# K read like V: 32 heads by four rows in 4 MB transfers, and a TensorE loop that branches to its slot

## Chip, cores and metric

One core of a Trainium2 chip runs the whole program. The metric is the device time of one execution in microseconds; the kernel before takes 214.04 us, the median of three runs.

## What is computed

A decode step with one query per sequence (batch 4): attention over a window of a K and V cache, plus a small MLP block on the same normalised input. Cut to what matters:

```python
B, D = 4, 576
Hq, Hkv, Sk, Dh, W = 32, 16, 8192, 128, 2048      # bf16
xn = layernorm(x)
q  = (xn @ wq).reshape(B, 32, 128)
k, v = k_cache[:, :, Sk-W:, :], v_cache[:, :, Sk-W:, :]   # 16 heads, each used by two query heads
p  = softmax(q . k / sqrt(128))                    # per query head, over 2048 rows
A  = (p @ v).reshape(B, 4096) @ wo
h  = gelu(layernorm(xn) @ w1)                      # sequence length 1: the shifts of h leave zeros
x1 = xn + shifted(h) @ w2
out = x + A + x1 + gelu(layernorm(x1) @ w3) @ w4
```

The K window is 4 x 16 x 2048 x 128 bf16, 33.55 million bytes, and V the same. With wq, wo, w1 to w4 the core reads 88.49 MB.

## The kernel before

**Engines and order.** Each engine runs a list written out ahead: `add(engine, emit, waits, sig, key)` puts an operation down, the lists are sorted by `key`, and an operation waits for named signals of others. TensorE has three such lists and two hardware loops between them: list `pe` (projections and MLP up to the hidden layer), the K loop (L653), list `pe2` (softmax's transposes), the V loop (L674), list `pe3` (output).

**DMA.** SP issues all large transfers from one list (L199, `add_dma`) in the order w1, w2, wq, w3, K, V, w4, wo. A transfer waits on SP for its slot to come free, and what stands behind it on SP waits too. Two buffers, `kring` (four slots of 2 MB and a rest) and `vring` (five slots of 2 MB), are shared by weights, K, V and the output weights in turn: wq lies in kring's second half until `q`, w3 in vring until `h2_1`.

**K.** `kv_src` reads K in 16 chunks of 2 MB, one sequence and four heads each: a partition row is 64 successive cache rows of one head, 16 KB. Four slots in kring; chunk c waits until the transposes of chunk c-4 are done. One turn of the K loop takes four chunks, one slot each, so that every instruction has its slot's address fixed; four turns.

For every chunk TensorE transposes 64 blocks of 128 x 128 (L485, eight to a PSUM bank, with `perm_bf` as the moving operand), VectorE (L469) and ScalarE (L468) copy the banks to `ktb` in the ratio 5 to 3, and TensorE multiplies (L492): four quarters by four heads, each 32 weight columns by 512 moving columns, written to one of four column groups of the array. The product of chunk c stands after the third block of chunk c+1. The weights are `Qs`, 128 columns that VectorE copies from `Qpad` for each chunk (L474). `Qpad` holds every head's two queries in its own columns with zeros beside them, so that the products of all chunks add up in four PSUM banks (`Sps`), which a zeroing of four products (L347) has prepared. All scores of the kernel stand there at the end, one partition for each query head of each sequence.

**Softmax.** VectorE takes the maximum over 2048 columns of PSUM (L498), ScalarE makes four exponentials of 512 columns (L502), VectorE transposes each in 32 x 32 blocks (L520), TensorE sorts them with 0/1 weights `pick_bf` in 64 products (L514), and two copies each on VectorE and ScalarE (L526, L529) put the result into `PT_t`.

**V.** Eight transfers of 4 MB, each with two sequences of 16 heads by four partitions: a partition row is 128 successive cache rows, 32 KB. Four slots: both halves of `vring`'s first 8 MB, then of kring's. VectorE spreads the probabilities (L545), TensorE multiplies (L553). The fifth transfer waits for the first's products, and so on; w4 waits for the sixth's products, wo for the fifth's and sixth's.

**End.** The products with w4 and wo (L392) are added up as the weights land, and two copies and one small DMA give the output.

Of the kernel before, what the change touches and what calls it, by code (L numbers as in the profile page):

```python
# [5 lines left out]
FP32 = mybir.dt.float32  # L6
# [8 lines left out]
N_LOOP = 4  # L15
N_CB = 4
# [21 lines left out]
def bass_parallel_sum__sliding_block_cached__mixer_s_mlp__decode_kernel(  # L38
# [16 lines left out]
    assert N_LOOP * N_CB == NC and LB % 4 == 0 and LB % NKT == 0  # L55
# [5 lines left out]
    CH = [(b, gq) for gq in range(4) for b in range(B)]  # L61
# [8 lines left out]
    with ExitStack() as ctx:  # L70
# [11 lines left out]
        kslot_t = lambda s: kslot(s).rearrange("p (t d) -> p t d", t=NT)  # L82
        vslot = lambda k: (vring, vring, kring, kring)[k][:, k % 2 * 2 * UE:(k % 2 + 1) * 2 * UE]
        ktbuf = ktb[:].rearrange("p (s t d) -> p s t d", s=NKT, t=8)
        ktgrp = ktb[:].rearrange("p (s t u i) -> p s t u i", s=NKT // 2, t=16, u=NU)
# [20 lines left out]
        PTx = vring[:, 4 * UE:4 * UE + 4 * 512].rearrange("p (q x) -> p q x", q=4)  # L106
# [22 lines left out]
        Qs = sb("Qs", [128, N_CB, 128], BF16)  # L129
        ident_bf = sb("ident_bf", [128, 128], BF16)  # L130
        perm_bf = sb("perm_bf", [128, 128], BF16)
        permT_bf = sb("permT_bf", [128, 128], BF16)
        pick_bf = sb("pick_bf", [128, 2 * NVS, 2, 32], BF16)
# [9 lines left out]
        negb = sb("negb", [128, 1], FP32)  # L143
        rs4 = sb("rs4", [128, 4], FP32)
# [11 lines left out]
        Sps = ps[:, 0:4, :]  # L156
# [21 lines left out]
        S["PV"] = sem("pv")  # L178
        S["FO"] = sem("fold")
# [57 lines left out]
        pool_ident(perm_bf, "perm_bf", [[-1, NU], [-NU, NI]], perm_bf[:].rearrange("p (u i) -> p u i", u=NU), -94)  # L237
        pool_ident(permT_bf, "permT_bf", [[-1, NI], [-NI, NU]], permT_bf[:].rearrange("p (i u) -> p i u", u=NU), -93)
        P(lambda e: e.memset(ktb[:, NKT // 2 * 1024:NKT * 1024], 0.0), key=-92, inc=(("E", LB - 2), 1))  # L239
        P(lambda e: e.memset(Qs[:, N_CB - 1, :], 0.0), key=-91, inc=(("E", LB - 1), 1))  # L240
        for j in (LB - 4, LB - 3):
            P(lambda e, j=j: e.sem_inc(S["E", j], 1), key=-90)
# [3 lines left out]
        P(lambda e: e.memset(pick_bf[:], 0.0), sig="pick0", key=-86)  # L246
        for gl in range(2):
            pick_v = pick_bf[:, :, gl, 16 * gl:16 * gl + 16]
            P(lambda e, v=pick_v: e.memset(v, 1.0), waits=["pick0"], sig=f"pick1{gl}", key=-85 + 0.1 * gl)
        for gl in range(2):  # L250
            for x in range(2 * NVS):
                v = pick_bf[:, x, gl, 16 * gl:16 * gl + 16].rearrange("p (u r) -> p u r", u=NU)
                P(lambda e, v=v, x=x: e.affine_select(out=v, in_=v, compare_op=ALU.is_equal, fill=0.0, base=-(8 * (x // 2) + x % 2),
                                                      pattern=[[-NI, NU], [-2, 4]], channel_multiplier=1),
                  waits=["pick11"], sig=f"pick2{gl}{x}", key=-84 + 0.1 * (8 * gl + x))
# [23 lines left out]
        def v_src(c, t0, t1):  # L279
# [5 lines left out]
        t_done = lambda c: f"T{NBLK * c + NBLK - 1}"  # L285
# [367 lines left out]
        with nc.Fori(0, N_LOOP, engines=[PE]) as it:  # L653
# [64 lines left out]
```

## Time and profile before

| | |
|---|---|
| median of three runs | 214.04 us (213.75 to 214.1) |
| the profiled execution | 213.93 us, of which the span from first to last instruction is 212.6 us |
| busy: TensorE, VectorE, ScalarE, GpSimd | 172.5, 111.9, 58.6, 15.6 us |
| bytes read | 88.49 MB, 416 GB/s over the span |
| K, V transfers | 16 of 2 MB; 7 of 4 MB and 2 of 2 MB |
| mean granted TensorE clock | 0.928 |

Lines below are those of the profile's page or of its views. A group's row has the kernel's line, engine, operation, what it writes and reads, shapes and count, then busy microseconds and mean nanoseconds of one, then idle time before it and what ended that. A row of the chain in order of time has start and duration in microseconds and what. A row of the view by windows has the stretch and its length, the busy time of TensorE, its weight loads, VectorE, ScalarE and GpSimd, the granted clock, the DMA engines' busy share and the GB/s. Matmuls overlap, so a mean of one is longer than the distance from one to the next.

### The profile page before, as it was taken

What the parts mean: (1) busy time and instruction counts of PE and PEld (TensorE: products, weight loads), DVE (VectorE), ACT (ScalarE), POOL (GpSimd) and SP (SyncE); (2) the same over time, 40 slices, a digit from 0 to 9 for tenths busy, and PEclk for the clock granted to TensorE, in tenths of its full rate; (3) what the DMA queues carried; (4) which work ended last, traced back from release to release, by engine and by line L of the source; (5) the groups of instructions that cost most, each with busy time, mean ns of one, the idle gap of its engine ahead of it and who ended that gap; (6) DMA issues with size and microseconds to landing.
All of it is one profiled execution on the core that took longest, in us unless ns stands there. A gap on an engine that the chain in (4) does not pass through costs nothing.

```text
span 212.6 us, 4856 instructions
## 1 busy us (share of the span) xinstructions
PE 172.5 (81%) x2212; PEld 133.7 (63%) x2216; DVE 111.9 (53%) x168; ACT 58.6 (28%) x69; POOL 15.6 (7%) x38
## 2 busy tenths in 40 slices
PE   1456147999999999999996089999989598997495
PEld 0222014888878888887774048988868487883262
DVE  5433200477776777777764869995575444003000
ACT  2004001366665566666656520000000000000000
POOL 8991000000000000000000000000000000000000
PEclk9997855899999999999999589999999889999799
DMA  6999999999999999999999999999999999999993
GB/s 242 453 444 445 429 396 416 432 425 427 429 416 438 432 422 429 435 422 424 432 444 438 444 407 459 413 425 453 407 444 438 419 425 410 451 476 393 407 408 131
DMA packets 5066, 88.65 MB, mean 417 GB/s; under 512 B 568, under 2 KB 704, under 8 KB 1216
## 3 DMA queue, kind: packets, MB, share of 16 engines
q1 hardware_dynamic: 5040, 88.49, 97.7%
q8 instruction: 8, 0.13, 0.3%
q14 instruction: 2, 0.02, 0.0%
q10 hardware_dynamic: 16, 0.01, 0.0%
HBM read 88.49 MB, written 0.00 MB: 416 GB/s over the span
## 4 chain that ended last, share of the span: by engine, by line
DMA 47%; PE 45%; DVE 4%; SPq 1%; ACT 1%; issue 1%
PE ps L485 23%; DMA vring<-in_A_wo_dram 15%; DMA vring<-in_B_w_dram 13%; DMA vring<-in_A_v_cache_dram 12%; PE ps L553 11%; DMA kring<-in_A_k_cache_dram 7%; PE ps L492 6%; PE ps L430 2%; SPq L199 1%; DVE vring L520 1%; DVE rmax L498 1%; DVE ktb L545 1%; PE ps L514 1%; PE ps L347 1%; ACT ktb L468 0%
## 5 line engine op out<-in xcount | busy, mean ns | idle before, releaser
L469 DVE COPY ktb<-ps 128x1024 bf16<-128x1024 bf16 x80 | 53.8, 689 | 23.5 <-PE ps L485 23.4
L485 PEld LDWEIGHTS ps<-perm_bf,kring 128*128 128x128 bf16 x1024 | 58.2, 98 | 8.3 <-issue 7.6
L485 PE MATMUL ps<-perm_bf,kring 128*128 128x128 bf16 x1024 | 61.7, 220 | 0.2
L468 ACT ACTIVATE ktb<-ps 128x1024 bf16<-128x1024 bf16 x48 | 48.0, 1023 | 32.5 <-PE ps L485 32.1
L545 DVE TENSOR_TENSOR ktb<-kring,mH_bf 128x4096 bf16<-128x4096 bf16 x16 | 36.2, 2286 | 14.6 <-PE ps L553 14.6
L553 PE MATMUL ps<-vring,ktb 128*128 128x256 bf16 x256 | 30.3, 282 | 4.3 <-DMA vring<-in_A_v_cache_dram 3.5
L553 PEld LDWEIGHTS ps<-vring,ktb 128*128 128x128 bf16 x256 | 25.7, 101 | 8.5 <-issue 3.6
L553 PE MATMUL ps<-kring,ktb 128*128 128x256 bf16 x256 | 28.6, 273 | 0.9 <-DMA kring<-in_A_v_cache_dram 0.9
L553 PEld LDWEIGHTS ps<-kring,ktb 128*128 128x128 bf16 x256 | 25.0, 98 | 4.5 <-issue 1.1
L608 ACT ACTIVATE out_sb<-ps 4x288 bf16<-4x288 f32 x1 | 0.4, 399 | 84.6 <-PE ps L392 84.6
L492 PE MATMUL ps<-ktb,Qs 128*32 128x512 bf16 x272 | 17.8, 382 | 1.2 <-ACT ktb L468 1.2
L430 PE MATMUL ps<-vring,xs 128*8 128x320 bf16 (+1 forms) x72 | 4.5, 429 | 7.6 <-DMA vring<-in_B_w_dram 7.6
L492 PEld LDWEIGHTS ps<-ktb,Qs 128*32 128x32 bf16 x272 | 5.7, 96 | 6.7 <-DVE ktb L469 1.4
L514 PE MATMUL ps<-vring,pick_bf 128*32 128x256 bf16 x64 | 3.9, 411 | 6.4 <-DVE rinv L532 6.4
L609 DVE CAST out_sb<-ps 4x288 bf16<-4x288 f32 x1 | 0.4, 449 | 15.7 <-PE ps L392 15.7
L392 PE MATMUL ps<-vring,h2T_sb 128*4 128x288 bf16 x72 | 6.2, 347 | 3.1 <-DMA vring<-in_B_w_dram 3.1
L571 DVE TENSOR_SCALAR tmp<-ps,maskd 128x128 f32<-128x128 f32 x2 | 0.7, 350 | 14.8 <-PE ps L553 14.8
L430 PEld LDWEIGHTS ps<-vring,xs 128*8 128x8 bf16 x72 | 2.1, 110 | 9.8 <-DMA vring<-in_B_w_dram 8.0
L330 PE MATMUL ps<-ident_bf,xp_bf 4*128 4x4 bf16 x15 | 0.8, 163 | 8.1 <-DVE xp_bf L314 5.0
L392 PEld LDWEIGHTS ps<-vring,h2T_sb 128*4 128x4 bf16 x72 | 3.7, 101 | 5.8 <-DMA vring<-in_B_w_dram 3.6
L514 PEld LDWEIGHTS ps<-vring,pick_bf 128*32 128x32 bf16 x64 | 2.0, 118 | 8.2 <-DVE rinv L532 6.9
L239 POOL MEMSET ktb<- 128x8192 bf16 x1 | 6.9, 6924 | 0.0
(93 smaller groups left out, 78.6 us busy)
## 6 DMA issues: line engine op xcount, KB each, us to landing
kring<-in_A_k_cache_dram SPq DMA_DIRECT2D x16, 2048.0 KB, 13.8
vring<-in_A_v_cache_dram SPq DMA_DIRECT2D x4, 4096.0 KB, 24.6
kring<-in_A_v_cache_dram SPq DMA_DIRECT2D x3, 4096.0 KB, 34.0
vring<-in_B_w_dram SPq DMA_DIRECT2D x2, 5184.0 KB, 25.1
kring<-in_A_wq_dram SPq DMA_DIRECT2D x1, 4608.0 KB, 15.7
kring<-in_A_v_cache_dram SPq DMA_DIRECT2D x2, 2048.0 KB, 27.4
vring<-in_A_wo_dram SPq DMA_DIRECT2D x1, 1872.0 KB, 26.9
vring<-in_A_wo_dram SPq DMA_DIRECT2D x1, 1440.0 KB, 29.8
```

The lines of the kernel that those rows point to most:

```text
L199: e.dma_start(o_, i_).then_inc(S[skey], 16)
L239: P(lambda e: e.memset(ktb[:, NKT // 2 * 1024:NKT * 1024], 0.0), key=-92, inc=(("E", LB - 2), 1))
L347: ins = e.matmul(ps[:, w, :], lhsT=zeros_bf[:, 0:128], rhs=zeros_bf[:, :], start=True, stop=True)
L392: return e.matmul(ACC[h], lhsT=lhsT, rhs=rhs, start=start, stop=stop, tile_position=(0, 32 * h), skip_group_check=True)
L430: ins = e.matmul(H2ps[k][32 * j:32 * j + 2 * B].rearrange("b (p t) -> b p t", t=n), lhsT=x_at(2, s_), rhs=w[:, :, 9 * j + t0:9 * j + t0 + ...
L468: return "act", lambda e: e.activation(out=ktbuf[:, n % NKT], in_=tb[n % 4], func=ACTF.Copy)
L469: return "dve", lambda e: e.tensor_copy(out=ktbuf[:, n % NKT], in_=tb[n % 4])
L485: ins = e.transpose(tb[j % 4][:, t, :], kslot_t(k)[:, 8 * kb + t, :], perm_bf[:])
L492: ins = e.matmul(Sps[32 * u:32 * u + 32, q, :].rearrange("p (t i) -> p t i", t=16), lhsT=Qs[:, k, 32 * u:32 * u + 32], rhs=ktgrp[:, (4 * k ...
L514: ins = e.matmul(ps[32 * j:32 * j + 32, 4 + qt, 256 * ih:256 * (ih + 1)].rearrange("p (t a e) -> p t a e", a=NPAIR, e=2), lhsT=pick_bf[:, ...
L545: return lambda e: e.tensor_tensor(out=PTpad[:, n % 4], in0=PTv[:, qt, NH * h:NH * (h + 1), bp, :].unsqueeze(2).to_broadcast([128, NH, NX, ...
L553: ins = e.matmul(ps[:, 0, 0:256], lhsT=PTpad[:, 2 * (k % 2) + h, 2 * g:2 * g + 2].rearrange("p t h e -> p (t h e)"), rhs=vslot(k)[:, Dh * ...
```

## The change

K is read in eight transfers of 4 MB in V's form: two sequences of 16 heads, four rows of partitions per head, 128 cache rows in each. The first comes in two halves. There are three slots instead of four: both halves of kring, and vring's second 4 MB, which w3 holds at first; so the third transfer waits for `h2_1`, later ones for the transposes of the third before. The second V transfer now waits for K's sixth to be transposed. A GpSimd operation for each landing counts up one semaphore, `KL`, for which the loop waits.

One turn of TensorE's loop is now one transfer, two halves of eight blocks; eight turns. Since three slots do not divide the turns evenly, the slot is a register (`k_at`), and each half of the body stands three times, once for each slot, chosen by two nested conditions. The score products stand once for each half: 32 heads, 32 weight columns by 256 moving columns, the weights taken from a buffer with all heads of two sequences (copied twice in the run instead of 16 times). The moving operand has runs of four elements, 256 bytes apart; eight rounds of four column groups add up in one half bank. VectorE takes each half's scores from PSUM to `S_sb`: a copy for the first two sequences, an addition for the others, and a maximum for each finished quarter. The zeroing before the loop goes.

In the softmax the exponentials read `S_sb`; VectorE's transposes and the 64 products go, and 40 products with full weights (`sel_bf`) of P itself put the probabilities in place: 32 of 128 columns, quarter by quarter, for two banks, and 8 of 512 columns for the other two banks, which only the second pair of sequences needs.

```diff
-N_LOOP = 4
-N_CB = 4
+N_LOOP = 8
+N_CB = 2
+NKS = 3
...
+        S_sb = vring[:, 4 * UE:4 * UE + 4096].bitcast(FP32).rearrange("p (q x) -> p q x", q=4)
-        kslot = lambda s: kring[:, s * UE:(s + 1) * UE]
+        kslot = lambda k: (kring[:, 0:2 * UE], kring[:, 2 * UE:4 * UE], vring[:, 2 * UE:4 * UE])[k]
-        ktgrp = ktb[:].rearrange("p (s t u i) -> p s t u i", s=NKT // 2, t=16, u=NU)
+        ktgrp = ktb[:].rearrange("p (s t h i) -> p s t h i", s=2, t=NT, h=NX)
...
-        def kv_src(cache, c):
-            b, gq = CH[c]
-            return cache[b, NU * gq:NU * gq + NU, Sk - W:Sk, :].rearrange("g (i t) d -> i g (t d)", t=NT)
...
+        def kv_src(cache, c, t0=0, t1=NTV):
             bp, qt = VCH[c]
             k0 = Sk - W + 4 * NTV * qt
-            return A_v_cache[2 * bp:2 * bp + 2, :, k0:k0 + 4 * NTV, :].rearrange(
+            return cache[2 * bp:2 * bp + 2, :, k0:k0 + 4 * NTV, :].rearrange(
                 "b h (i t) d -> (b h) i (t d)", t=NTV)[:, :, Dh * t0:Dh * t1]
...
-        for c in range(NC):
-            w = [t_done(c - N_CB)] if c >= N_CB else (["q"] if c >= 2 else [])
-            add_dma([(kslot(c % N_CB), kv_src(A_k_cache, c))], ("k", c % N_CB), w, c)
+        t_done = lambda c: f"T{2 * NBLK * (c + 1) - 1}"
+        for c in range(NCK):
+            w = [t_done(c - NKS)] if c >= NKS else ([], ["q"], ["h2_1"])[c]
+            for n, (u0, u1) in enumerate([(0, NH), (NH, NTV)] if c == 0 else [(0, NTV)]):
+                ev_k = add_dma([(kslot(c % NKS)[:, Dh * u0:Dh * u1], kv_src(A_k_cache, c, u0, u1))], ("k", c % NKS) if n == 0 else "k0b", w, c + 0.1 * n)
+                if n == 0:
+                    P(lambda e: e.sem_inc(S["KL"], 1), waits=[ev_k], key=c)
         for c in range(NCV):
-            w = [f"PV{2 * (c - NVS) + 1}"] if c >= NVS else [t_done(NC - N_CB + 2 * c - 3)] if c >= 2 else ["h2_1"]
+            w = [f"PV{2 * (c - NVS) + 1}"] if c >= NVS else [t_done(NCK - NVS + c)] if c else ["h2_1"]
...
-        add("pe", pe_zero, waits=["h2T"], sig="s_zero", key=-9.5)
+        add("dve", lambda e: e.tensor_copy(out=Qs, in_=Qpad_t[:, 0:1024]), waits=["qT3"], sig="Qs0", key=0)
+        add("dve", lambda e: e.tensor_copy(out=Qs, in_=Qpad_t[:, 1024:2048]), waits=[f"SC{NC // 2 - 1}"], key=NB // 2 + NBLK - 0.4)
...
-                ins = e.transpose(tb[j % 4][:, t, :], kslot_t(k)[:, 8 * kb + t, :], perm_bf[:])
+                ins = e.transpose(tb[j % 4][:, t, :], kslot(k)[:, Dh * (8 * j + t):Dh * (8 * j + t + 1)], ident_bf[:])
...
-            for q in range(4):
-                for u in range(NU):
-                    ins = e.matmul(Sps[32 * u:32 * u + 32, q, :].rearrange("p (t i) -> p t i", t=16),
-                                   lhsT=Qs[:, k, 32 * u:32 * u + 32], rhs=ktgrp[:, (4 * k + q) % (NKT // 2), :, u, :],
-                                   start=False, stop=False, tile_position=(0, 32 * u), skip_group_check=True)
+            for h in range(NX):
+                u = h % NU
+                ins = e.matmul(ps[32 * u:32 * u + 32, k, 0:256].rearrange("p (t i) -> p t i", t=NT),
+                               lhsT=Qs[:, 32 * h:32 * h + 32], rhs=ktgrp[:, k, :, h, :],
+                               start=(h < NU), stop=(h >= NX - NU), tile_position=(0, 32 * u), skip_group_check=True)
...
+        S_at = lambda c: S_sb[:, c % 8 // 2, 256 * (c % 2):256 * (c % 2 + 1)]
+        for c in range(NC):
+            last = c == NC - 1
+            w, key = (["SCend"], KS) if last else ([f"SC{c}"], NBLK * (c + 2) - 0.5)
+            if c < NC // 2:
+                add("dve", lambda e, c=c: e.tensor_copy(out=S_at(c), in_=ps[:, c % 2, 0:256]), waits=w, key=key)
+            else:
+                add("dve", lambda e, c=c: e.tensor_tensor(out=S_at(c), in0=S_at(c), in1=ps[:, c % 2, 0:256], op=ALU.add), waits=w,
+                    sig="S_last" if last else f"S{c}", key=key)
+                if c % 2:
+                    add("dve", lambda e, c=c: e.tensor_reduce(out=rm4[:, c % 8 // 2:c % 8 // 2 + 1], in_=S_sb[:, c % 8 // 2, :], axis=AX.X, op=ALU.max),
+                        waits=["S_last" if last else f"S{c}"], sig="rm4" if last else None, key=key + 0.01)
...
-        def pe_PT(qt):
+        def pe_PT(q0, q1, x):
             def f(e):
                 ins = None
+                for i in range(4):
+                    ins = e.matmul(ps[:, 4 + x, 128 * q0:128 * q1].rearrange("p (q t) -> p q t", t=128), lhsT=sel_bf[:, x, 3 - i:131 - i],
+                                   rhs=P_sb[:, q0:q1, 128 * i:128 * (i + 1)], start=(i == 0), stop=(i == 3), skip_group_check=True)
                 return ins
             return f
...
         with nc.Fori(0, N_LOOP, engines=[PE]) as it:
             turn = e.snap(it + 1)
-            landed = e.snap(16 * it + 16)
+            k_at = e.snap(it * 32 - ((it * 11) & 96) * NKS, min_val=0, max_val=64)
 
             def wait(j):
-                if j % NBLK == 0:
-                    e.wait_ge(S["k", j // NBLK], landed)
+                if j == 0:
+                    e.wait_ge(S["KL"], turn)
+                if j == NBLK:
+                    e.wait_ge(S["k0b"], 16)
                 e.wait_ge(S["E", (j - 4) % LB], turn)
-            for j in range(LB):
-                emit_T(e, j, wait)
-                if j % NBLK == 2:
-                    k = (j // NBLK - 1) % N_CB
-                    e.wait_ge(S["E", NBLK * k + 6], turn)
-                    e.wait_ge(S["E", NBLK * k + 7], turn)
-                    emit_SC(e, k).then_inc(S["SC"], 1)
+
+            def half(h, k):
+                for j in range(NBLK * h, NBLK * (h + 1)):
+                    emit_T(e, j, wait, k)
+            for h in range(2):
+                with e.If(k_at < 32):
+                    half(h, 0)
+                with e.Else():
+                    with e.If(k_at < 64):
+                        half(h, 1)
+                    with e.Else():
+                        half(h, 2)
+                k = 1 - h
+                for x in (6, 7):
+                    e.wait_ge(S["E", NBLK * k + x], turn)
+                emit_SC(e, k).then_inc(S["SC"], 1)
```

More of the change, by code (lines that the diff above doesn't have):

```diff
@@ L342, in x_at @@
             return xs_t[:, idx, 2 * B * (s_ + 1):2 * B * (s_ + 2)]
-        def pe_zero(e):
-            ins = None
-            for w in range(4):
-                ins = e.matmul(ps[:, w, :], lhsT=zeros_bf[:, 0:128], rhs=zeros_bf[:, :], start=True, stop=True)
-            return ins
         ln_ops(0, x_sb, xn_bf, [ev_x], "ln1", -40)
@@ L472, in bass_parallel_sum__sliding_block_cached__mixer_s_mlp__decode_kernel @@
             c, k = n // NBLK, n % NBLK
-            if k == 0:
-                add("dve", lambda e, c=c: e.tensor_copy(out=Qs[:, c % N_CB, :], in_=Qpad_t[:, 128 * (4 * CH[c][0] + CH[c][1]):][:, 0:128]),
-                    waits=[f"SC{c - 2}"] if c >= 1 else ["qT3"], key=n)
             eng, f = evac(n)
```

89 lines of the change are left out of this document (40 added, 49 removed).

## Prediction

> **What bounds the kernel now.** I read the page's top and its DMA part first, then the DMA view cut to two stretches, then the chain that ended last, in order of time.
>
> ```profile
> span 212.6 us, 4856 instructions
> DMA  6999999999999999999999999999999999999993
> q1 hardware_dynamic: 5040, 88.49, 97.7%
> q8 instruction: 8, 0.13, 0.3%
> ```
>
> The 16 DMA engines are over 90% busy in every slice but the first and the last; 97.7% of the span on the one data queue leaves about 5 us, which is the start and the end. Everything read is 88.49 MB, and the change reads the same bytes. So the span is: a start, 88.49 MB at the engines' pace, an end. A faster compute engine gains nothing. There are two ways to move the time: make the engines move the bytes faster, or let them run dry.
>
> The chain, in order of time (start, duration, what):
>
> ```profile
> 2.17 27.46 DMA vring<-in_B_w_dram
> ...
> 35.49 0.32 DVE h2T_sb L452
> 35.81 0.45 issue
> 36.26 1.49 PE ps L347 x3
> ...
> 44.38 0.98 PE ps L492 x16
> 45.36 3.71 PE ps L485 x64
> ...
> 94.51 14.58 DMA kring<-in_A_k_cache_dram
> ...
> 115.17 1.07 PE ps L492 x16
> 116.27 2.30 DVE rmax L498
> ...
> 118.78 0.79 ACT Qpad L502 x2
> 119.59 2.72 DVE vring L520 x4
> ...
> 122.62 2.05 PE ps L514 x32
> 124.70 0.69 DVE kring L526
> 125.39 2.21 DVE ktb L545
> ...
> 127.73 7.16 PE ps L553 x64
> ...
> 142.08 25.49 DMA vring<-in_A_v_cache_dram
> ...
> 178.35 31.68 DMA vring<-in_A_wo_dram
> ```
>
> The chain is named 45% TensorE, but look at the three DMA pieces: 14.58, 25.49 and 31.68 us from issue to landing. 4 MB (4.194 million bytes) at about 0.43 MB/us take 9.75 us, so these transfers stood in a queue. The chain passes through their issue, yet an issue some microseconds later would have been absorbed by that queue. These waits are the slack that the change may spend.
>
> **The transfers.** K goes from 16 pieces of 2 MB, 16 KB in each partition row, to 4 MB transfers of 32 KB a row, the form that V has already; K's first 4 MB stay in two halves of 16 KB rows. The DMA view of 40 to 100 us (K alone) and of 117 to 175 us (V alone) tells what each form costs; columns are packets, MB, and share of 16 engines' time:
>
> ```profile
> q1 hardware_dynamic: 1752, 25.56, 100.2%
> ```
> ```profile
> q1 hardware_dynamic: 852, 24.85, 99.7%
> ```
>
> K: 1.002 x 60 us x 16 engines / 25.56 MB = 37.63 engine-us per MB. V: 0.997 x 58 x 16 / 24.85 = 37.23. The difference is 0.40 / 16 = 0.025 us per MB. Seven of the eight new transfers, 29.36 MB, get it: 29.36 x 0.025 = 0.73 us. The shares are rounded to 0.1%, worth 0.07 us, and K's stretch held one instruction fetch more. The other end is from the throughput of the same two stretches:
>
> ```profile
> 40.00:100.00 60.00, 59.95 (x1028) 50.08 (x1017) 43.75 (x77) 37.63 (x39) 0.00 (x0) 1.00 1.01 427
> 117.00:175.00 58.00, 48.03 (x445) 40.27 (x447) 40.53 (x30) 3.98 (x10) 0.00 (x0) 0.91 1.00 429
> ```
>
> 29.36/0.427 - 29.36/0.429 = 0.32 us. I take the middle, **-0.5 us**, bounds -0.3 to -0.7. All of it lies on the path, as long as the queue never runs dry. The rest of this part is about that.
>
> **TensorE's loop.** Before, one 2 MB chunk takes 3.71 (64 transposes, L485) + 0.98 (16 score products, L492) = 4.69 us against 2.097/0.427 = 4.91 us for its bytes. After, half a transfer is again 64 transposes, and moving identity instead of a permutation costs the same. The 32 score products have 256 columns where 16 had 512: the same columns, twice the weight loads, and the moving operand is now read in runs of four elements, 256 bytes apart, where it was runs of 32. Low bound 0.98. High bound from the nearest row with 256 columns, four column groups and short runs (two elements), at the full clock:
>
> ```profile
> 123.99 2.52 PE L514 MATMUL ps<-vring,pick_bf 128*32 128x256 bf16 x40
> 124.30:126.10 1.80, 1.80 (x39) 0.97 (x32) 1.00 0.89 382
> ```
> ```profile
> 31.78 2.17 PE L430 MATMUL ps<-vring,xs 128*8 128x320 bf16 x36
> 29.70:33.70 4.00, 4.00 (x68) 2.09 (x72) 0.50 1.03 438
> L430 PE MATMUL ps<-vring,xs x72: 397/422/457, 29.7 to 33.8; 128*8 128x320 bf16 x36, 128*8 128x256 bf16 x36
> L514 PE MATMUL ps<-vring,pick_bf x64: 390/412/415, 122.6 to 126.1; 128*32 128x256 bf16 x64
> ```
>
> L514: ten rounds of four, (2.52 - 0.41)/9 = 0.234 us a round, at full clock; eight rounds and a start of 0.12 make 2.0 us. L430's second half is 256 columns in runs of four, (2.17 - 0.42)/8 = 0.219 at *half* the clock, one 320-column round included: runs of four are at least as fast at half the clock as runs of two at the full one. If a run has a price, it is 0.234/128 = 1.8 ns, and 64 runs make 0.117 us a round, the time that the columns need anyway. I take 8 x 0.117 + 0.12 = **1.06 us**, bounds 0.98 and 2.0. The Trainium skill (SBUF — State Buffer, Door 1, its note on lines) says that SBUF is read in 16-byte lines, that a line should be hit at least twice, and that each step to a new line costs a penalty without giving a price. By it every run here pays, and the sum would go towards the 2.0 us; the L514 row agrees, the L430 row bounds it.
>
> **The branches.** The loop turn is seen in the trace:
>
> ```profile
> L653 PEldq ALU_OP  x4: 32/32/32, 56.1 to 113.0; - x4
> L653 PEldq COMPARE_BRANCH  x4: 76/212/238, 56.2 to 113.1; - x4
> 54.66 3.75 PE L485 MATMUL ps<-perm_bf,kring 128*128 128x128 bf16 x64
> ```
>
> A taken branch holds the sequencer 0.21 to 0.24 us, one not taken 0.08. The turn starts at 56.1, while the products of the next iteration follow after 40 of that run of 64, at 54.66 + 40 x 0.058 = 57.0. The sequencer is thus 0.9 us ahead, and the run shows no gap: 0.9 us of queued products is the cover. After, a half has up to two taken compares and a jump out; a turn adds some five register operations (about 0.1 each with what lies between) and the old turn. That is 0.3 to 0.7 in the middle of an iteration, hidden, and 1.1 to 1.6 at a turn, of which 0.3 to 1.1 shows. Without the cover it would be about 1 us a half. Spread over two halves I take 0.35: a half costs 3.71 + 1.06 + 0.35 = **5.1 us** (4.9 to 6.0).
>
> **When the queue would run dry.** The loop starts at 35.81 plus the copy of all queries (at most the 0.69 us of the evacuation of like size, below), 36.6; the zeroing of 36.26 (1.49 us) goes. K ends at 36.6 + 16 x 5.1 + 1.1 = 119.3, or, since the last 4 MB must land whole (29.6 + 8 x 9.75 = 107.6, then two halves), at 118.9: about 3 us later than 116.25. Softmax to first V product took 127.73 - 116.25 = 11.5. After: last add, maximum of one quarter, maximum and scale about 1.3 (before 2.45), four exponentials 2.7 as now; the four DVE transposes (2.72) and 64 pick products go, 40 selector products come, of which 16 follow the last exponential, some 4.3 at half the clock, with the mask product beside it. About 8.6, bounds 8 and 11.5. First V product at 128 (127 to 131): even. The fifth V transfer is issued 7.16 us after, at 135 as now; it must be there before the fourth lands, 167.57 - 2 x 9.75 = 148.1. Slack 12 us, or 0.75 us a half: **a half may cost 5.7 to 5.8 us before DMA sees it.** K's own slots are looser: transfer c+3 is issued at 36.6 + 5.1 x 2(c+1) and due at 29.6 + 9.75(c+3), with 10 us to spare. The transfers behind the changed waits on SP's queue (second on the queries, third and first V on the hidden layer at 34) are issued with 8 MB still ahead of them.
>
> VectorE: 5 evacuations and, new, a score copy or add in place of the query copy:
>
> ```profile
> L469 DVE COPY ktb<-ps 128x1024 bf16<-128x1024 bf16 x80 | 53.8, 689 | 23.5 <-PE ps L485 23.4
> L474 DVE COPY Qs<-Qpad 128x128 bf16<-128x128 bf16 x16 | 2.9, 183 | 0.0
> L526 DVE CAST kring<-ps 128x512 bf16<-128x512 f32 x2 | 1.4, 686 | 1.8 <-PE ps L514 1.8
> L537 DVE COPY rinvB<-ps 128x128 f32<-128x128 f32 x1 | 0.3, 281 | 0.0
> ```
>
> 256 floats lie between 0.28 and 0.69, 0.42; with a quarter's maximum now and then 5 x 0.69 + 0.42 + 0.2 = 4.1 us a half, under 4.9. The score copy waits for the products behind which the next evacuation stands, but that evacuation waits for a later transpose anyhow. GpSimd's new relay of each landing adds a few tenths before a half; it is idle then. Sum: -0.5 us for the bytes, 0 for the rest.
>
> **Rivals.** *TensorE is too slow* (slower): the score products cost L514's 2.0, and turns add 0.3: 6.0 us a half, 0.2 to 0.4 over the limit, 16 x 0.2 to 0.4 = 3 to 6 us, minus 0.5: 216.5 to 219.5. From 5.8 us a half it decides, and each further 0.1 costs 1.6 us. For it: run length and the doubled weight loads. Against: L430. *Jumps miss* (slower): forward jumps wait for code. The loop turn shows only jumps back, and the body grows from 320 to some 480 pairs of load and product. Eight instruction packets of 16 KB in the whole run say that four passes did not fetch again. If the longer body did, each half would wait for about one fetch, for which the nearest row is the landing of the smallest weights (columns: KB, us to landing):
>
> ```profile
> ktb<-in_B_w_dram SPq DMA_DIRECT2D x2, 648.0 KB, 4.3
> ```
>
> At 3 to 4.3 us a fetch a half costs 8 to 9.4 us, 2.3 to 3.6 over the limit, and the time is some 250 to 270. The Trainium skill (Runtime: NRT & Kernel Launch, Instruction fetch mechanics) states that a taken branch to a target outside the loaded pages stalls for a fetch; the turn's 0.21 us shows no such stall for a jump of the whole old body. *No gain* (same): the K stretch is slower for what else runs in it, not for its row length, or the transfers are cut as before: 214.0.
>
> **How the numbers follow.** The profiled execution took 213.93 beside its span of 212.6; the median of three is 214.04, and I apply the sum to it: 213.5. Chances: forecast 0.62 (213.2 to 213.8; 0.48 of it beyond 0.43 us, the 0.2% that a measurement of this kernel can tell, 0.14 within), no gain 0.10 (0.08 within, 0.02 faster), TensorE too slow 0.16, jumps miss 0.07, some other starving of the queue, 214.5 to 218, 0.05. Faster 0.50, same 0.22, slower 0.28. Range 212.9 to 217.5: the gain's bound and some noise below, most of the first rival above; about 0.12 lies above it, 0.04 below.
>
> **What would show it.** DMA tenths all 9 and the data queue near 97.5% of a shorter span: right. A digit under 9 between 40 and 180 us: the queue ran dry. Score products near 1.06 and a half near 5.1 with idle time at the turns: steps right; K's transfers at the V form's 37.2 engine-us per MB: gain right. Many more than eight packets on the instruction queue, or microseconds of issue time ahead of L485's successor, would make it wrong.

## The result, and the profile after

| | before | after |
|---|---|---|
| median | 213.99 us (213.75 to 214.21, six runs) | 220.97 us (219.96 to 222.82, six runs) |
| ratio | | 1.034, interval 1.029 to 1.039 |
| the profiled execution | 213.93 us, span 212.6 | 222.57 us, span 221.2 |

The change costs 7.0 us. The forecast was 213.5, range 212.9 to 217.5. The profiled execution of after lies 1.6 us above its median, so the account below is of 222.57 - 213.93 = 8.6 us.

The page of after, in the same parts as were shown of before, with the throughput of the slices:

```profile
span 221.2 us, 5425 instructions
DMA  7999989999993998999999999998999999999892
GB/s 287 388 465 435 465 376 453 412 447 403 455 403 145 367 403 344 415 403 450 403 456 416 444 427 427 456 394 326 397 441 421 439 433 400 473 409 472 367 416 100
q1 hardware_dynamic: 4032, 88.49, 94.4%
q8 instruction: 9, 0.15, 0.3%
```

The same bytes took 94.4% of a longer span. Between 40 and 200 us the row leaves its nines at three places: the 3 in the slice of 66 to 72 us (145 GB/s), the 8 at 83 to 88 us (344 GB/s), and the 8 at 149 to 155 us (326 GB/s). At the first no data packet ran at all for 2.4 us; at the other two some of the 16 DMA engines had run out of work while others still had some. What that cost is read from the stretches (columns as before), first of after, then of before:

```profile
40.00:60.00 20.00, 11.50 (x150) 10.25 (x152) 5.74 (x9) 5.12 (x5) 0.00 (x0) 0.76 0.99 422
60.00:80.00 20.00, 19.69 (x367) 17.34 (x360) 13.70 (x23) 10.93 (x11) 0.00 (x0) 0.94 0.80 332
80.00:100.00 20.00, 19.85 (x388) 17.62 (x386) 15.06 (x26) 12.36 (x13) 0.00 (x0) 1.00 0.96 392
100.00:120.00 20.00, 19.73 (x381) 17.21 (x379) 15.35 (x26) 11.98 (x13) 0.00 (x0) 1.00 1.00 428
140.00:160.00 20.00, 19.49 (x156) 15.73 (x156) 19.21 (x14) 2.78 (x4) 0.00 (x0) 0.89 0.93 387
```
```profile
60.00:80.00 20.00, 20.00 (x347) 16.98 (x345) 14.82 (x26) 12.73 (x13) 0.00 (x0) 1.00 1.01 429
80.00:100.00 20.00, 19.95 (x340) 16.61 (x338) 14.74 (x27) 12.72 (x14) 0.00 (x0) 1.00 1.00 427
140.00:160.00 20.00, 18.93 (x170) 16.37 (x170) 13.66 (x8) 0.00 (x0) 0.00 (x0) 1.00 1.01 433
```

In 60 to 100 us, (429 - 332 + 427 - 392) x 20 us = 2.64 MB fewer, at 0.43 MB/us 6.1 us. In 140 to 160, (433 - 387) x 20 = 0.92 MB, 2.1 us. Together 8.2 of the 8.6 us. The column of the DMA engines' busy share splits this: 0.21 x 20 + 0.04 x 20 = 5.0 us and 0.08 x 20 = 1.6 us are engines without work, and the remaining 1.6 us are packets that took longer. The first row shows where it began: 40 to 60 has full throughput, but TensorE was busy for 11.5 of 20 us, at a granted clock of 0.76.

The chain in order of time, from the start of TensorE's loop:

```profile
36.95 6.09 PE ps L473 x64
43.04 3.16 issue
46.20 1.90 PE ps L480 x32
48.09 5.63 PE ps L473 x64
53.94 5.34 issue
59.28 1.90 PE ps L480 x31
61.18 4.28 PE ps L473 x64
...
76.97 3.68 PE ps L473 x64
80.65 1.26 PE ps L480 x31
81.91 3.68 PE ps L473 x64
...
127.35 3.81 PE ps L473 x64
131.16 2.56 PE ps L480 x51
...
135.30 4.86 ACT Qpad L501 x8
140.20 1.05 PE ps L510 x8
```

L473 are the transposes, L480 the score products. The first pass holds two waits for nothing that the profile shows ("issue"), 3.16 and 5.34 us; no later pass has one of this size. From 61.18 to 127.35 thirteen halves take 66.2 us, 5.09 us a half. The first pass took 61.18 - 36.95 = 24.2 us for two: 14.0 us too many. Of these 8.5 are the waits, and 5.6 are slow products: transposes at 6.09 and 5.63 instead of 3.7 and score products at 1.90 instead of 1.26, at a granted clock of 0.59 in 36.9 to 43.0, 0.62 in 46.2 to 54.0 and 0.75 in 59.3 to 65.4 us. The first 2.4 of the 5.6 lie ahead of both waits. They belong to the start of the loop and not to the jumps, as the kernels below without a wait at this place show: their first 64 transposes took 5.0 to 6.4 us. In e7, with the score products behind them:

```profile
36.63 5.36 PE L473 MATMUL ps<-ident_bf,kring 128*128 128x128 bf16 x64 [1.03 <-DVE kring L453]
41.92 1.33 PE L480 MATMUL ps<-ktb,kring 128*32 128x256 bf16 x32
```

The waits and the slow products behind them are thus 11.7 us. The sequencer's row for the outer condition (minimum, median, maximum in ns):

```profile
L667 PEldq COMPARE_BRANCH  x22: 73/208/4055, 36.6 to 126.2; - x22
```

One of 22 took 4.06 us. It is the jump out of the first half, at 41.83 us, over the two other slots' code. An instruction packet landed at 44.50 and the products went on at 46.20; in the second wait one landed at 57.71 and they went on at 59.28. The second wait is not at a jump: the compare ahead of it (52.58 us) took 0.29 us, and the wait stands behind the first of the 32 score products, in code that follows in line. The profile ties no packet to a wait; that TensorE stood without code both times is read from these times, and the next section tests it. SP's list shows what waited for it:

```profile
53.76 17.20 SPq L199 DMA_DIRECT2D kring<-in_A_k_cache_dram  x2
80.68 0.54 SPq L199 DMA_DIRECT2D vring<-in_A_k_cache_dram  x1
90.56 10.61 SPq L199 DMA_DIRECT2D kring<-in_A_k_cache_dram  x2
...
152.32 7.69 SPq L199 DMA_DIRECT2D vring<-in_A_v_cache_dram  x2
```

The first row's second issue, K's fifth transfer, came at 70.4, when the second transfer's transposes were done; the fourth had landed whole at 69.3 by its packets, and the fifth's first packet started at 71.8. The fifth V transfer came at 152.3, when engines had already run out of the fourth, whose last packet ended at 154.1: the last of the three places.

### The profile page after: what moved, and what is told of

Read it like the earlier page. It is cut to its first block, busy times and chain, and to the rows that moved or that the text cites. A ratio compares the mean times of both kernels' runs of the same rounds, so it can differ in the third digit from the quotient of the medians.

```text
span 221.2 us, 5425 instructions
## 1 busy us (share of the span) xinstructions
PE 181.5 (82%) x2457; PEld 147.0 (66%) x2460; DVE 115.2 (52%) x170; ACT 63.4 (29%) x69; POOL 13.6 (6%) x29
## 3 DMA queue, kind: packets, MB, share of 16 engines
q1 hardware_dynamic: 4032, 88.49, 94.4%
## 4 chain that ended last, share of the span: by engine, by line
PE 62%; DMA 25%; issue 5%; ACT 3%; DVE 3%; SPq 1%; DVEq 0%
PE ps L473 29%; PE ps L550 19%; DMA vring<-in_B_w_dram 12%; DMA vring<-in_A_wo_dram 12%; PE ps L480 10%; ACT Qpad L501 2%; PE ps L421 2%; SPq L199 1%; DVE ktb L542 1%; ACT kring L526 1%; PE ps L510 0%; PE ps L434 0%; PE ps L561 0%; PE ps L383 0%; DVE rm L495 0%
## 5 line engine op out<-in xcount | busy, mean ns | idle before, releaser
L473 PE MATMUL ps<-ident_bf,kring 128*128 128x128 bf16 x768 | 50.1, 231 | 1.8 <-DVE kring L453 1.5
L473 PEld LDWEIGHTS ps<-ident_bf,kring 128*128 128x128 bf16 x768 | 47.9, 104 | 5.6 <-issue 5.3
L480 PE MATMUL ps<-ktb,kring 128*32 128x256 bf16 x544 | 24.0, 322 | 8.5 <-issue 8.5
L480 PEld LDWEIGHTS ps<-ktb,kring 128*32 128x32 bf16 x544 | 14.6, 104 | 13.8 <-issue 9.1
L473 PEld LDWEIGHTS ps<-ident_bf,vring 128*128 128x128 bf16 x256 | 14.3, 98 | 1.9 <-issue 1.8
L473 PE MATMUL ps<-ident_bf,vring 128*128 128x128 bf16 x256 | 15.1, 219 | 0.6 <-issue 0.6
L490 DVE COPY vring<-ps 128x256 f32<-128x256 f32 x8 | 3.4, 425 | 13.2 <-PE ps L480 13.2
L510 PE MATMUL ps<-Qpad,sel_bf 128*128 128x128 bf16 (+1 forms) x40 | 7.0, 353 | 3.8 <-ACT Qpad L501 3.8
L510 PEld LDWEIGHTS ps<-Qpad,sel_bf 128*128 128x128 bf16 x40 | 3.9, 132 | 6.5 <-ACT Qpad L501 4.9
L492 DVE TENSOR_TENSOR vring<-vring,ps 128x256 f32<-128x256 f32 x8 | 3.4, 422 | 7.0 <-PE ps L480 7.0
```

Source lines behind the costliest of these rows:

```text
L473: ins = e.transpose(tb[j % 4][:, t, :], kslot(k)[:, Dh * (8 * j + t):Dh * (8 * j + t + 1)], ident_bf[:])
L480: ins = e.matmul(ps[32 * u:32 * u + 32, k, 0:256].rearrange("p (t i) -> p t i", t=NT), lhsT=Qs[:, 32 * h:32 * h + 32], rhs=ktgrp[:, k, :, ...
L490: add("dve", lambda e, c=c: e.tensor_copy(out=S_at(c), in_=ps[:, c % 2, 0:256]), waits=w, key=key)
L492: add("dve", lambda e, c=c: e.tensor_tensor(out=S_at(c), in0=S_at(c), in1=ps[:, c % 2, 0:256], op=ALU.add), waits=w, sig="S_last" if last ...
L510: ins = e.matmul(ps[:, 4 + x, 128 * q0:128 * q1].rearrange("p (q t) -> p q t", t=128), lhsT=sel_bf[:, x, 3 - i:131 - i], rhs=P_sb[:, q0:q1 ...
```

## The experiments

Two theories follow. *Cold code*: the first pass of the branching loop waits for code, which spends more slack than the slots have. *Too much else*: even without the waits the new order is slower, by its score products or its softmax. The kernels are numbered e1 to e12; all but e3, e6 and e10 start from after. Before, measured again beside each group of them, took 213.96 to 214.04 us.

**The K loop written out (e1).** TensorE's 16 halves stand in line, with fixed slots and no jump; the products are the same.

```diff
-with nc.Fori(0, N_LOOP, engines=[PE]) as it:
+for it in range(N_LOOP):
...
-    with e.If(k_at < 32): half(h, 0)   # and the two others
+    emit_T(e, j, wait, it % NKS)       # for the eight blocks of the half
```

> The changed kernel with TensorE's K code written out as 16 halves in a row: no loop, no branch, the rest as it is. Cold code (my theory: only the first pass of the branching loop stalls, 3.2 + 5.3 us and slow products after, and that delays the issues of the fifth K transfer and the fifth V transfer past the queue's end): no stall over 1 us before the second half, K's products end near 118 to 122 us, DMA busy throughout, time 213.3 to 214.3. Rival A (the score products or the three slots are too slow as such): a half stays near 5.1 us, K ends near 130 or DMA still runs dry after the fourth K transfer, time 217 or more. Rival B (32 KB rows are slower in K's place): K's engine time per MB stays above 37.6, time above 214.5.

Measured: 216.21 us (216.0 to 216.91), ratio 1.010 (1.008 to 1.011). The page:

```profile
DMA  6999999999999999999999999999999999998970
q8 instruction: 17, 0.28, 0.5%
```

No stall, no dry place, and 4.8 us of the 7.0 are gone: cold code is right for these. But 2.24 us stay, with the queue full until the last slices, and no theory had them. Rival B asked for K packets over 37.6 engine-us per MB; a 32 KB packet took 1.22 us, which is 37.2.

**Three transfers in a turn (e2).** A loop whose turn is three transfers, one for each slot, needs no condition. Two turns and two transfers in line.

```diff
-with nc.Fori(0, N_LOOP, engines=[PE]) as it:   # slot chosen by conditions
+with nc.Fori(0, 2, engines=[PE]) as it:
+    for s_ in range(NKS): k_turn(it * NKS + (s_ + 1), s_)
+for s_ in range(2): k_turn(2 * NKS + s_ + 1, s_)
```

> The changed kernel with TensorE's K loop as two turns of three transfers, one for each slot, and two more transfers written out behind it: a loop, jumps back only, no conditions. Cold code: the same as the straight version, 213.3 to 214.3, with up to 1 us of stall at the one jump back and less code fetched. Rival A: 217 or more. If any jump in the loop were the cost, a stall of 3 us or more would stand at the second turn, near 67 us, and the time would lie 0 to 2 us above the straight version.

214.88 us (214.84 to 215.08), ratio 1.0044 (1.003 to 1.006), no dry slice, 13 instruction packets. The jump back to code that has run held the sequencer for 0.24 us (70.8 us) and left no wait of TensorE. The time is again over the range that cold code gave, 213.3 to 214.3; the two kernels differ mainly in how much code there is.

**The ninth skipped (e7).** Three turns of three, and one condition that leaves the last out.

```diff
+with nc.Fori(0, 3, engines=[PE]) as it:
+    for s_ in range(2): k_turn(it * NKS + (s_ + 1), s_)
+    third = e.snap(it + 0)
+    with e.If(third < 2): k_turn(it * NKS + 3, 2)
```

> The turn-of-three version without the two transfers written out behind the loop: a third turn, of which a condition skips the third transfer. 600 to 800 instructions less code. Theory of the code packets: 10 of them instead of 13, 213.9 to 214.2. Rival (no cost per packet): as turn-of-three, 214.7 to 215.1.

214.66 us (214.36 to 215.04), ratio 1.003 (1.002 to 1.004): the best of the new order, still 0.7 us slower than before. It is 0.5 above the range of the theory of code packets and 0.04 below the range of the rival, so e2 and e7 alone give a packet little or no price. Against after, 6.3 of the 7.0 us are gone.

```profile
DMA  6999999999999999999999999999999999999991
q8 instruction: 10, 0.16, 0.3%
```

**The first turn in line, the others in the branching loop (e5).** All slots' code is then met by jumps in the second turn.

```diff
+for h in range(2):
+    k_half(h, 0, wait_at(1)); k_score(h, 1)
-with nc.Fori(0, N_LOOP, engines=[PE]) as it:
+with nc.Fori(1, N_LOOP, engines=[PE]) as it:
```

> The changed kernel with its first turn written out ahead of the loop, and seven turns left in the branching loop. Cold code: the long exit jump (4.06 us in the changed kernel's first turn) moves to the loop's new first turn, near 47 to 58 us; TensorE is late again by 5 to 9 us, but one transfer further on, where the fifth K transfer is still issued before the fourth has landed (69 us), so K does not run dry; about 10 or 11 code packets. Time 214.5 to 217, most below the changed kernel. Rival (steady cost of branches and products, 5.1 us a half, decides): as the changed kernel, 220 to 222.

218.31 us (218.15 to 219.26), ratio 1.021 (1.019 to 1.0235). The stall went with the first forward jump, as cold code says, and the row of the condition shows its price again, beside TensorE's idle time behind it:

```profile
L677 PEldq COMPARE_BRANCH  x18: 77/208/4967, 46.9 to 121.4; - x18
```
```profile
59.96 5.16 PE L473 MATMUL ps<-ident_bf,kring 128*128 128x128 bf16 x64 [4.09 <-issue]
```

A jump of 4.97 us at 54.7, and the jump out of the next half (64.1 us) took 1.17. The fifth K transfer was issued at 65.2, 4.1 us ahead of the fourth's last packet, and K had no dry place. The fifth V transfer came at 147.6, 2.1 us ahead of the fourth's last packet (149.7). That was too late for most engines: at 148.5 to 149 us only 2 of 16 had a packet, and the slice fell to 269 GB/s. The expectation ended 1.3 us too low: the late V was not in it.

**What a dry queue costs (e3, e4).** In the kernel before, K's ninth transfer waits for the transposes of the seventh chunk instead of the fifth, and nothing else is changed; in the straight kernel K's fifth transfer waits for 18 blocks more (the second block of the fourth transfer).

```diff
-w = [t_done(c - N_CB)] if c >= N_CB else ...               # before
+w = [t_done(c - 2 if c == 8 else c - N_CB)] if c >= N_CB else ...
...
-w = [t_done(c - NKS)] if c >= NKS else ...                 # straight
+w = (["T49"] if c == 4 else [t_done(c - NKS)]) if c >= NKS else ...
```

> The kernel before with one K transfer (the ninth) issued late: it waits for the transposes of the seventh chunk instead of the fifth, so that the queue runs dry for 2.5 to 3.5 us near 69 us; nothing else changes. If a dry queue costs only its idle time: 216.5 to 217.5. If the restart is slow as well, as the changed kernel's packets of 1.3 to 2.3 us after its dry spot suggest (1.22 us undisturbed): 218 to 221, with 16 KB packets well over 0.62 us for 10 to 20 us.

> The straight version with one K transfer (the fifth) issued late: it waits for the second block of the fourth transfer's transposes, so that the queue runs dry for 2 to 3 us near 69 us. Idle time only: 2 to 3 us over the straight version. Slow restart: 5 to 8 us over it, with 32 KB packets of 1.3 us and more until about 95 us, and K's throughput in 70 to 90 us near 340 instead of 430 GB/s. With the changed kernel's first dry spot this alone should bring most of its loss back.

The first: 217.86 us (217.48 to 218.58), 3.9 more than before. Its slices:

```profile
DMA  6999999999995799999999999999999999989893
GB/s 261 439 437 466 420 397 425 425 430 428 428 419 217 274 425 419 431 434 433 428 437 464 404 458 410 449 416 431 434 416 446 416 452 392 491 380 481 366 415 118
```

It lies between the two expectations. The execution with this trace took 218.58, 4.6 more than before, though no data packet ran for only 2.9 us (69.5 to 72.4). The second: 222.41 us (221.92 to 223.32), 6.2 more than the straight kernel, as a slow restart would have it, but with 4.4 us without a data packet (69.8 to 74.2) where 2 to 3 were planned; its traced execution took 222.34. The stretches of 66 to 70, 70 to 76 and 76 to 82 us, first of e3, then of e4:

```profile
66.00:70.00 4.00, 4.00 (x71) 3.24 (x69) 2.96 (x6) 2.28 (x4) 0.00 (x0) 1.00 0.48 205
70.00:76.00 6.00, 5.74 (x99) 4.81 (x96) 4.55 (x8) 3.97 (x5) 0.00 (x0) 1.00 0.62 235
76.00:82.00 6.00, 3.39 (x40) 1.96 (x40) 1.66 (x4) 1.82 (x2) 0.00 (x0) 0.81 1.00 426
```
```profile
66.00:70.00 4.00, 4.00 (x82) 3.64 (x75) 2.75 (x6) 2.46 (x3) 0.00 (x0) 1.00 0.44 184
70.00:76.00 6.00, 6.00 (x126) 5.22 (x127) 4.66 (x8) 3.82 (x5) 0.00 (x0) 1.00 0.33 101
76.00:82.00 6.00, 5.68 (x120) 4.71 (x108) 3.96 (x7) 3.62 (x4) 0.00 (x0) 1.00 0.99 423
```

The DMA share gives the engines' idle time: 0.52 x 4 + 0.38 x 6 = 4.4 us in e3, 0.56 x 4 + 0.67 x 6 = 6.3 us in e4, beside 4.6 and 6.1 us lost. So idle time is nearly the whole price, once each engine is counted: the 16 engines do not run out together, the first of them some 2 us ahead of the last. The slow restart falls: the first packet or two of each engine are long (1.8 to 2.2 us for 32 KB in e4), but from 76 us on the throughput is 423 GB/s again, not 340. In after, the idle engines at 82 to 86 us (0.84 busy) fit the late sixth transfer, issued at 80.7, 2.3 us ahead of the fifth's last packet (83.0); this part was not tried alone.

**The old order, written out (e6).** Before's own K loop in line, nothing else: more code, no new order.

```diff
-with nc.Fori(0, N_LOOP, engines=[PE]) as it:
-    turn = e.snap(it + 1)
+for it in range(N_LOOP):
+    turn, landed = it + 1, 16 * it + 16
```

> The kernel before with its K loop written out: four times the code, nothing else. Theory (each 16 KB packet of code that the core fetches costs the end about 0.3 us, because the packets go through one of the 16 engines and that engine finishes last; from straight +9 packets and turn-of-three +5 packets, after 0.5 us for the rows): 15 to 16 code packets, 216.0 to 216.5, the engines' shares in the last microseconds uneven. Rival (the extra time of the straight and turn-of-three versions is from the 4 MB transfers or the three slots): 213.8 to 214.3.

215.39 us (215.27 to 215.59), ratio 1.0064 (1.005 to 1.008), between the two. Its page has 15 instruction packets instead of eight:

```profile
q8 instruction: 15, 0.25, 0.5%
```

1.43 us for seven packets of 16 KB is 0.20 us each, five times what 16 KB need at 0.43 MB/us (0.04). Writing the loop out was the only change, so more code beside a full data queue costs time here. How it does is shown in part. A code packet took about 1.05 us of one engine, and the data packet that started as it ended took about 0.5 us more than usual (in e1 1.7 us instead of 1.22); 1.55 us of one engine is 0.10 us of all 16, half of the 0.20. The other pairs do not give the same price: 0.33 us for each of the four packets between e1 and e2, 0.07 for each of the three between e2 and e7. At 0.20 the straight kernel's nine packets more than before are 1.8 us, most of what it kept.

**Row length by itself (e9).** The kernel with the skipped ninth, with all K transfers in two halves of 16 KB rows.

```diff
-enumerate([(0, NH), (NH, NTV)] if c == 0 else [(0, NTV)])
+enumerate([(0, NH), (NH, NTV)])
```

> The kernel with three turns of three transfers and a skipped ninth, in which now every K transfer is issued in two halves of 16 KB rows, as the first one was; all else as it was (214.66 us with 32 KB rows). It sets the row length apart from the rest of the change. Theory: 32 KB rows move a 4 MB transfer in 9.71 us where 16 KB rows took 9.79; seven transfers lose 0.5 to 0.6 us, so 215.2 us (215.0 to 215.4), with steady pitches of 9.78 to 9.83 us per 4 MB of K. Rival: the longer row brings nothing that reaches the end (the last engine is late for another reason, and a longer packet is a coarser piece at the end of each transfer): 214.5 to 214.75, or earlier.

215.22 us (214.95 to 215.37), ratio 1.0052 (1.004 to 1.0065), against 214.66. The longer rows are worth 0.56 us, at the end too. The stretch of 40 to 100 us, first with 16 KB rows, then with 32 KB:

```profile
40.00:100.00 60.00, 60.00 (x1154) 53.09 (x1152) 44.08 (x73) 36.98 (x36) 0.00 (x0) 0.99 1.01 427
```
```profile
40.00:100.00 60.00, 57.62 (x1079) 51.34 (x1077) 41.60 (x69) 34.62 (x34) 0.00 (x0) 0.97 1.00 430
```

427 and 430 GB/s. With before's rows the new order is thus 1.24 us slower than before, with two packets more (0.4 us at e6's price, 0.1 to 0.7 by the spread of the pairs). Some 0.8 us are left. One place where they may lie is the end: in w4's transfer the last packet ends at 199.77 where the one before it ends at 198.46 (32 KB rows; 200.31 and 199.24 with 16 KB rows); in before it is 198.84 and 198.69.

**Is it the late issue (e10)?** Before, with w4 waiting for one half of products more.

```diff
-"w4", [f"PV{2 * (NCV - NVS + 1) + 1}"], KS + NCV)
+"w4", [f"PV{2 * (NCV - NVS + 2)}"], KS + NCV)
```

> The kernel before, with one wait changed: w4's transfer waits for one more half of V products (the first half of the seventh V transfer) and is issued at about 179 to 180 us instead of 176.6; the five transfers of wo stand behind it on SP. The queue still has the eighth V transfer's 4 MB, so it does not run dry. In all kernels with the new K order w4 is issued at 178.1 to 178.7, and their last DMA engine ends 0.9 to 1.5 us behind the mean engine where before it was 0.8 behind. Theory A: less work ahead in the engines' own queues makes their ends uneven, and this costs 0.3 to 0.9 us: 214.3 to 214.9. Theory B: the time of issue does not matter as long as the queue has work, and the uneven end comes from the instruction packets alone: 213.9 to 214.1.

214.03 us (213.66 to 214.35) against 213.98, with w4 issued at 181.0 us instead of 176.6: no effect, as theory B has it for the time of issue.

**Is it where the last code packet falls (e11, e12)?** In the kernel with the skipped ninth an instruction packet ends at 197.78 us, and w4's last packet starts at 197.77; the trace names no engine, but the times fit one engine that had both. Eight and 24 small products ahead of the K loop move all later code, the second three times as far as the first.

```diff
+for _ in range(8):    # 24 in the other
+    e.matmul(ps[:, 6, 0:64], lhsT=zeros_bf[:, 0:128], rhs=zeros_bf[:, 0:64], start=True, stop=True)
```

> The kernel with three turns of three transfers and a skipped ninth (214.66 us), with eight added small products (64 columns of zeros) on TensorE just before the K loop: about half a microsecond, ten microseconds ahead of any need, and every later instruction of TensorE moves by 1 KB within the 16 KB pieces in which its code is fetched. Theory: the 0.9 us by which that kernel's last DMA engine ends later than before is one instruction packet that lands at 196.7 us on an engine with w4's last piece still to move (that engine ends w4 at 199.77 where the next ends at 198.46); with the code moved, the packet comes at another time and on another engine, and the time changes by 0.3 us or more, down to 213.6 or up to 215.2. Rival: the late end is a fixed cost of the new order: 214.5 to 214.8, with the last engine again some 0.8 us behind the mean.

> The same with 24 such products: 3 KB further. Theory: again another time and engine for each late instruction packet, and a time that differs from that of the other shifts by 0.3 us or more where the packet falls on an engine that would have ended early, 213.5 to 213.8 (a little faster than before, since the row length brings 0.56 us and two packets more take 0.2 to 0.4). Rival: 214.5 to 214.8 in both.

214.71 (214.46 to 215.87) and 214.75 us (214.53 to 215.29). The theory falls. In the second the packet's start moved from 196.7 to 161.7 us, and still one engine ended w4 1.2 us behind the next (199.84, 198.68). The 0.8 us stay open.

**The exponentials in order (e8).** The skipped-ninth kernel, with the exponentials reading the scores in the order in which they lie; the probabilities then stand in another order.

```diff
-in_=S_sb[:, q, :].rearrange("p (t i) -> p i t", i=4), func=ACTF.Exp
+in_=S_sb[:, q, :].rearrange("p (i t) -> p i t", i=4), func=ACTF.Exp
```

> As skip-ninth, with the exponentials reading the scores in order instead of regrouped by four (the order of P is then another; nothing else is left out). Theory (the step of 16 bytes between successive reads makes the exponential 1.19 instead of 0.69 us, and with it two of the three microseconds by which softmax took longer than forecast): L501 near 0.69, the first V product 2 us sooner after the last score product; time unchanged within 0.5 us, since nothing waits for it. Rival (reading SBUF instead of PSUM costs it): L501 stays at 1.19.

214.52 us in one run. The row of the exponentials, first of the skipped-ninth kernel, then of this one:

```profile
L501 ACT ACTIVATE Qpad<-vring,negb 128x512 bf16<-128x512 f32 x4 | 4.8, 1192 | 1.8 <-DVE negb L498 1.8
```
```profile
L501 ACT ACTIVATE Qpad<-vring,negb 128x512 bf16<-128x512 f32 x4 | 2.8, 709 | 1.8 <-DVE negb L498 1.8
```

Reading SBUF in both cases, a step of 16 bytes between successive values took 1192 ns where successive ones took 709. The first V product came 1.2 us sooner after the last score product (9.8 us instead of 11.0), not 2. As the queue is full then, the time stays within the 0.5 us that was expected; one run can say no more.

## Why the prediction was wrong

- **Jumps: the step that failed.** The prediction had two cases, a body that does not fetch again (nothing) and one that misses in each half (250 to 270 us), and gave the second 0.07. It took the loop turn, a jump back, as its row. The case between was left out: in the first pass a forward jump goes over code that nobody has run yet. After's first pass waited twice, 8.5 us of TensorE's time, and behind the waits, at a low clock, products took 3.2 us more: 11.7 us that the sum put at nothing. A second term was too small at the same place: the first 64 transposes took 6.09 us and not 3.71, 2.4 us more; in the kernels without a wait there they were too slow as well (5.0 to 6.4). Together that is 14.0 us, while the prediction's own limits were 10 us at K's slots and 12 at the fifth V transfer. The fifth K transfer was issued at 70.4 where its sum gives 57.0. Its price for a fetch, 3 to 4.3 us, was near the 4.06 measured; but two of them, 6 to 8.6 us, would still have fitted under 10 us. Without the slow products behind the waits the fifth transfer would have been issued at about 67 us by these rows, ahead of the fourth's last packet (69.3). The Trainium skill (Runtime: NRT & Kernel Launch, Instruction fetch mechanics) says that a taken branch to a page that isn't loaded stalls; the first jump agrees. The page gives TensorE room for 2048 instructions, and in a note says that only two pieces of 256 are held. By the note the later passes, over 448 pairs of load and product (the prediction said some 480), would stall each time; the row of L667 with its median of 208 ns, and no 16 KB instruction packet between 72.5 and 148.9 us, show that they do not. By the larger figure only the first pass can miss, and that is what happened.
- **A half costs 5.1 us: right** (5.09), by luck in part: two errors cancel. The score products take 1.26 us, not 1.06 (bounds 0.98 and 2.0), and what lies between the groups is some 0.1 a half, not 0.35. The note on lines in the Trainium skill (SBUF — State Buffer, Door 1) may have part of its due: 1.26 lies 0.28 over before's 0.98, the same columns read in long runs. But there are also twice the weight loads, and no run sets the two apart.
- **Rows of 32 KB, -0.5 us: right in size** (0.56 between e9 and e7), and lost in the sum.
- **Code beside data: not in the sum.** The prediction counted instruction packets to see whether the loop misses, and gave a packet no price. By e6 each costs 0.20 us. After has nine, one more than before, so this is small in the kernel as changed, but it takes back most of the gain or more in the forms that avoid the stall.
- **Softmax to the first V product, 8.6 us: mis-sized.** It took 11.4 (from the last score product at 133.72 to 145.13), near the end of the range, 11.5. The exponentials were carried over at 0.69 us each, though they now read another layout; they took 1.19, and the four 4.86 us instead of 2.7. Ahead of them it was 1.6 us instead of 1.3, behind them 5.0 instead of 4.3, if the 4.3 holds the copy and the spreading as well (only so do its terms add up to 8.6). By e8 the layout accounts for 1.2 us of the 2.8.
- **The fifth V transfer at 135 us:** 152.3 in after, 137.8 to 141.6 in the kernels of the new order without a stall or a delayed transfer, which show no dry slice ahead of the end. But the limit of 148 was too late: at 147.6 (e5) the queue already thinned out, since the limit is when the last engine runs out and not the first.
- **A microsecond of dry queue costs a microsecond:** assumed by the rival's arithmetic. It holds for the engines' mean idle time (e3, e4), and is too cheap if only the stretch without any packet is counted.
- **The rivals.** "TensorE is too slow" (216.5 to 219.5) ends 1.5 us below the measured time, and its cause was another: behind the first pass no half came to 5.8 us. "No gain" is near where the best form without the stall ends, 0.7 us above before.
- **What was to show it** did in two of three signs: a digit under 9 between 40 and 180 us, and microseconds of issue time in the loop, ahead of L480. The third, many more than eight instruction packets, did not come: nine, so the count does not tell this case.

Open: some 0.8 us that the new order costs with the same rows, no dry place and two code packets more. Delaying w4 in the old order did not bring them, and moving the late code in the new one did not take them away. Not tried: which DMA engine takes which code packet, and the three slots, GpSimd's counting of landings and the changed waits of V each by itself.

## What to carry to other kernels

Ahead of a loop with branches, price its first pass apart: a forward jump over code that has not run waits for a fetch, and the slack of the buffers has to hold that wait together with the slow clock after it. A buffer's slack ends when the first DMA engine runs out, here some 2 us ahead of the last. When a kernel is bound by its data queue, count code as traffic: give each further 16 KB of instructions its measured price (0.2 us in the cleanest pair here, 0.07 to 0.33 in others) against the microsecond that a better layout brings. A row of the old kernel prices an operation only in the layout that it had.

## What the runs showed of the hardware

- A first forward jump held the sequencer for 4.06 us (after) and 4.97 us (e5) beside a full data queue; in after, products went on 1.6 to 1.7 us after a code packet had landed. The same jumps later took about 0.2 us.
- A packet of 16 KB of code took about 1.05 us, and the 32 KB data packet that started as it ended took about 1.7 us instead of 1.22 (e1).
- The 16 DMA engines do not run out together: 2.9 us without any data packet went with 4.4 us of mean idle time (e3), 4.4 with 6.3 (e4).
- Behind such a stretch the first 32 KB packets took 1.6 to 2.2 us instead of 1.22 (after, e4), and the throughput was back at 423 GB/s from 76 us on (e4).
- An exponential of 128x512 took 1192 ns reading SBUF with a step of 16 bytes between float values, and 709 ns in order (e7, e8).
